# Cutting the last load of values of a decode attention kernel at 1/2 and 7/8 instead of 1/2 and 3/4

## The chip, the cores and the metric

The kernel runs on one core of one Trainium2 chip. The metric is the device time of one execution in microseconds (us). Times of a pair are compared within the same rounds on the same chip. Times inside an execution are counted from the start of its profiled span and rounded to hundredths, so a difference of two of them can be off by 0.01 us. The profile models the ends of matmuls; the starts of matmuls and of the casts behind them are recorded.

## The reference

```python
xn = _layernorm(x)                                   # x: 2 x 1 x 448, bfloat16
q  = (xn @ wq)                                       # 16 query heads of 256, 8 key/value heads
k, v = caches[:, :, Sk - 4096:, :]                   # the last 4096 of 32768 positions
p  = softmax(q k^T * 256 ** -0.5)
out = x + (p @ v) @ wo + mish_mlp(xn)                # one query position in each of 2 sequences
```

For each of 8 key/value heads and 2 sequences, 2 MB of keys and 2 MB of values are read once: 16 "heads" in the words of the kernel. With the weights some 78 MB are read for an output of 1.8 KB.

## The kernel before

Partition p holds 32 consecutive positions (T = 32) of 256 elements, that is 16 KB of keys and 16 KB of values per head. The loads stand in one queue, issued by SyncE. The parts here are the last head's values, the output weights `wo` behind them, and the products that use both.

```python
def load_v(i, cuts=(0, T)):                          # one load per part
    ...
    for lo, hi in zip(cuts, cuts[1:]):
        nc.sync.dma_start(out=t[:, lo:hi, :], in_=vin[:, lo:hi, :])

def load_wo(kvh, parts=1):                           # 448 KB for two query heads
    ...
    for u in range(parts):
        hs = slice(u * rep // parts, (u + 1) * rep // parts)
        nc.sync.dma_start(out=w[:, hs, :], in_=win[:, hs, :])

def values_fixed(i):                                 # the last four heads
    ...
    for t in range(T):                               # 2 matmuls for each t: 64 in all
        for c in range(ND):
            nc.tensor.matmul(po[:, c, :], lhsT=vv[:, t, c, :], rhs=pTv[:, th, 0:Q:HS], ...)
    scale_o(i, po)                                   # VectorE: oT = o / denominator

def mix(kvh):                                        # 16 matmuls, 8 for each query head h
    for h in range(rep):
        for c in range(ND):
            add(oT[:, c, h, :], w[:, h, c * D : (c + 1) * D], ...)

for i in range(NK + KA):                             # NK = 16 heads
    if i + 2 < NK:
        load_k(i + 2)
    if i < NK:
        load_v(i, (0, T) if i < NK - 1 else (0, T // 2, 3 * T // 4, T))
        ...
        if b == Bsz - 1:
            load_wo(kvh, parts=1 if i < NK - 1 else 2)
    ...

for n in range(NO):                                  # the close: four casts, one store
    copy = nc.vector.tensor_copy if n // 2 == 0 else nc.scalar.copy
    copy(out=res[:, n * DO : (n + 1) * DO], in_=part(n))
nc.sync.dma_start(out=out.flatten_outer_dims(), in_=res[:])
```

The softmax here doesn't subtract the row's maximum and nothing guards it: scores larger than these inputs give would overflow.

Of the kernel before, what the change touches and what calls it, by code (L numbers as in the profile page):

```python
# [34 lines left out]
def kernel(  # L35
# [26 lines left out]
    T = W // P  # L62
# [40 lines left out]
    def v_tile(n):  # L103
        t = v_pool.tile([P, T * Dh], BF16, tag="v", name="v")
        return t[:, 0:n]
# [150 lines left out]
    def build_q(i):  # L256
        kvh, b = heads[i]
        x, h0 = divmod(kvh * rep, HH)
        t = qdiag[i % NW]
        tv = t[:].rearrange("p (n e) c -> p n e c", e=NE)  # L260
        for j in range(NQ):
            rows = slice(j * Q, (j + 1) * Q)
            for e in range(NE):
                nc.gpsimd.tensor_copy(  # L264
                    out=tv[rows, :, e, j * Q : (j + 1) * Q : HS],
                    in_=qrep[rows, :, h0 : h0 + rep, e, x, b],
                )
# [56 lines left out]
    def dense_out():  # L324
        w2_sb = dense.pop("w2")
        for x in range(NX):
            for c in range(NF):
                add(act_bf[:, c, x, :], w2_sb[:, x, c, :])
# [6 lines left out]
    def load_k(i):  # L335
        kvh, b = heads[i]
        t = k_pool.tile([P, T * Dh], BF16, tag="k", name="k")
        nc.sync.dma_start(  # L338
            out=t[:], in_=A_k_cache[b, kvh, s0:Sk, :].rearrange("(p t) d -> p (t d)", p=P)
        )  # L340
        k_t[i] = t

    def load_v(i, cuts=(0, T)):
        kvh, b = heads[i]
        t = v_tile(T * Dh).rearrange("p (t d) -> p t d", t=T)
        vin = A_v_cache[b, kvh, s0:Sk, :].rearrange("(p t) d -> p t d", p=P)
        for lo, hi in zip(cuts, cuts[1:]):
            nc.sync.dma_start(out=t[:, lo:hi, :], in_=vin[:, lo:hi, :])
        v_t[i] = t

    def load_wo(kvh, parts=1):
        w = wo_pool.tile([P, rep, ND * D], BF16, tag="wo", name="wo")
        r0 = kvh * rep * Dh
        win = A_wo[r0 : r0 + rep * Dh, :].rearrange("(h p c) d -> p h (c d)", h=rep, p=P)
# [3 lines that stand above are left out]
        wo_t[kvh] = w  # L358

    def turn(s):  # L360
        kt = kt_pool.tile([P, TH * Dh], BF16, tag="kt", name="kt")
        i, half = divmod(s, NH)
        k = k_t[i] if half < NH - 1 else k_t.pop(i)
        nc.vector.transpose(  # L364
            out=kt[:].bitcast(FP32),
            in_=k[:, half * TH * Dh : (half + 1) * TH * Dh].bitcast(FP32),
        )
        kt_t[s] = kt

    def scores(s):  # L370
        i = s // NH
        ktv = kt_t.pop(s)[:].rearrange("p (t n c e) -> p n e t c", t=TH, n=NB, e=NE)
        psc = ps_sc.tile([P, TH, Q], FP32, tag="sc", name="sc")
        for n in range(NB):
            for e in range(NE):
                nc.tensor.matmul(  # L376
                    psc[:],
                    lhsT=qdiag[i % NW][:, n * NE + e, :],
                    rhs=ktv[:, n, e, :, :],
                    start=(n == 0 and e == 0),  # L380
                    stop=(n == NB - 1 and e == NE - 1),
                )
        p_sb = p_pool.tile([P, TH * Q], BF16, tag="p", name="p")
        if s % NH == 0:
            state["rs", i] = small.tile([P, NH], FP32, tag="rs", name="rs")
        nc.scalar.activation(  # L386
            out=p_sb[:],
            in_=psc[:].rearrange("p t c -> p (t c)"),
            func=ACT.Exp,
            scale=scale,  # L390
            accum_out=state["rs", i][:, s % NH : s % NH + 1],
        )
        p_t[s] = p_sb

    def turn_p(s):
        pT = p_pool.tile([P, TH * Q], BF16, tag="pT", name="pT", bufs=7)
        nc.vector.transpose(out=pT[:], in_=p_t.pop(s)[:])  # L397
        pT_t[s] = pT
        i, half = divmod(s, NH)
        if half != NH - 1:  # L400
            return
        rs = state.pop(("rs", i))
        sums = small.tile([P, rep], FP32, tag="sums", name="sums", bufs=4)
        nc.vector.tensor_scalar(  # L404
            out=sums[:], in0=hsel, scalar1=rs[:, 0:1], scalar2=None, op0=ALU.mult
        )
        nc.vector.scalar_tensor_tensor(  # L407
            out=sums[:], in0=hsel, scalar=rs[:, 1:2], in1=sums[:], op0=ALU.mult, op1=ALU.add
        )
        state["sums", i] = sums  # L410
# [13 lines left out]
    def values(i):  # L424

        po = ps_o.tile([NR, NP * Dh], FP32, tag="o", name="o")
        v = v_t.pop(i)
        state["rec", i] = denominator(i)
        for u in range(T // NP):
            half, uh = divmod(u, TH // NP)  # L430
            nc.tensor.matmul(  # L431
                po[:],
                lhsT=pT_t[i * NH + half][:, uh * NP * Q : (uh + 1) * NP * Q : HS],
                rhs=v[:, u * NP : (u + 1) * NP, :].rearrange("p t d -> p (t d)"),
                start=(u == 0),
                stop=(u == T // NP - 1),
            )
        o_sb = small.tile([NR, NP * Dh], FP32, tag="o_sb", name="o_sb", bufs=1)
        nc.scalar.copy(out=o_sb[:], in_=po[:])  # L439
        state["o", i] = o_sb  # L440
# [28 lines left out]
    def values_fixed(i):  # L469

        state["rec", i] = denominator(i)
        pq = ps_q.tile([P, NP * ND * NR], FP32, tag="q", name="q")
        po = pq[:, 0 : ND * rep].rearrange("p (c h) -> p c h", c=ND)
        vv = v_t.pop(i).rearrange("p t (m c) -> p t c m", c=ND)
        for t in range(T):
            half, th = divmod(t, TH)
            pTv = pT_t[i * NH + half][:].rearrange("p (t c) -> p t c", t=TH)
            for c in range(ND):
                nc.tensor.matmul(  # L479
                    po[:, c, :],  # L480
                    lhsT=vv[:, t, c, :],
                    rhs=pTv[:, th, 0:Q:HS],
                    start=(t == 0 and c == 0),
                    stop=(t == T - 1),
                    skip_group_check=True,
                )
        scale_o(i, po)
# [12 lines left out]
    NK = len(heads)  # L500
# [11 lines left out]
    def close(i):  # L512
        if i < NK - NFIX:
            finish(i)
        kvh, b = heads[i]
        if b == Bsz - 1:
            mix(kvh)

    for i in range(NK + KA):
        if i + 2 < NK:  # L520
            load_k(i + 2)
        if i < NK:
            load_v(i, (0, T) if i < NK - 1 else (0, T // 2, 3 * T // 4, T))
            kvh, b = heads[i]
            if b == Bsz - 1:
                load_wo(kvh, parts=1 if i < NK - 1 else 2)
            for half in range(NH):
                s = i * NH + half
                if s + 1 < NSTEP:
                    turn(s + 1)  # L530
                scores(s)
                if s >= 1:
                    turn_p(s - 1)
                if s == NSTEP - 1:
                    turn_p(s)
                if half == 0 and i > KA:
                    close(i - KA - 1)
            if i + 2 < NK:
                build_q(i + 2)
        if i == NK:  # L540
            close(i - KA - 1)
        if i == 0:
            dense_in()
        if i == 1:
            dense_out()
        if i >= KA:
            if i - KA < NK - NFIX:
                values(i - KA)
            else:
                values_fixed(i - KA)  # L550
        if i >= NK:
            close(i - KA)
# [37 lines left out]
```

## Time and profile before

| | before |
|---|---|
| time, first three runs | 190.46 us median (190.43 to 190.48) |
| profiled span | 188.7 us |
| DMA | 77.86 MB at a mean of 413 GB/s |
| last values landed | 184.27 us |
| second half of the last wo landed | 185.44 us |
| first cast | 185.86 us |

The first three rows are in the results and on the page. A landing is the last of the sixteen semaphore increments of a load, as the trace records it. The chain that ended last, from the trace of the kernel before (start us, length us, what), ran like this at the end:

```profile
158.66 25.61 DMA v<-in_A_v_cache_dram
184.27 0.05 issue
184.31 0.60 PE q L479 x16
184.91 0.02 issue
184.94 0.18 DVE oT L447
185.11 0.04 issue
185.16 0.79 PE psA L214 x15
185.94 0.23 ACT res L557
186.18 0.27 ACTq L585
```

This goes from the last values through their 16 matmuls, the scaling and the wo products to the close, and puts everything from 184.27 on the path. But the wo products stand as one piece of 0.79 us, and a wait inside that piece does not show. The prediction finds it in the timeline.

### The profile page before, as it was taken

The page shows a single profiled execution, that of the slowest core. Times are in us where ns is not written, and L with a number is a line of the kernel's source. Part 1 is how long each engine was busy: PE and PEld are TensorE (multiplying, and loading weights), DVE is VectorE, ACT ScalarE, POOL GpSimd, SP SyncE. Part 2 cuts the span into 40 slices and gives each one's busy share as a digit, 9 for nine tenths or more (in the row PEclk, how much of TensorE's full clock was granted, in tenths as well). Part 3 has the DMA queues.
Part 4 walks back from the last instruction along what each step waited for, and adds up shares of the span by engine and source line. Part 5 has one row for each costly group of instructions (what it writes and reads, how often), then busy time and mean ns, then how long its engine had stood idle before and what let it go on. Part 6 is the DMA issues. An engine that isn't in the chain of part 4 may idle for free.

```text
span 188.7 us, 2944 instructions
## 1 busy us (share of the span) xinstructions
PE 144.1 (76%) x1158; PEld 71.7 (38%) x1158; DVE 113.5 (60%) x195; ACT 32.5 (17%) x82; POOL 27.1 (14%) x139
## 2 busy tenths in 40 slices
PE   0152991788995799869985999769986999597782
PEld 0042390234442345334432434324533443254671
DVE  7805505997919392857649381939376673939401
ACT  2300110112212022111222112202311121211101
POOL 8004430033030022003030203003110300000000
PEclk9999995799999699988999699969998799969955
DMA  6999999999999999999999999999999999999991
GB/s 216 423 432 422 430 430 434 438 431 420 417 441 431 420 416 438 441 427 405 442 434 429 434 420 431 434 431 420 431 431 438 412 432 434 431 441 417 408 394 49
DMA packets 7816, 77.86 MB, mean 413 GB/s; under 512 B 757, under 2 KB 2809, under 8 KB 3322
## 3 DMA queue, kind: packets, MB, share of 16 engines
q1 hardware_dynamic: 7796, 77.66, 97.3%
q8 instruction: 9, 0.15, 0.3%
q14 instruction: 5, 0.04, 0.1%
q10 hardware_dynamic: 6, 0.01, 0.0%
HBM read 77.67 MB, written 0.00 MB: 412 GB/s over the span
## 4 chain that ended last, share of the span: by engine, by line
DMA 82%; DVE 11%; issue 2%; PE 2%; SPq 1%; ACT 0%; ACTq 0%
DMA k<-in_A_k_cache_dram 68%; DMA v<-in_A_v_cache_dram 14%; DVE kt L364 8%; DVE pT L397 2%; PE sc L376 1%; SPq L114 0%; PE psA L214 0%; SPq L338 0%; PE q L479 0%; SPq L280 0%; DVE sums L407 0%; SPq L275 0%; DVE sums L404 0%; DVE den_sb L320 0%; ACT p L386 0%
## 5 line engine op out<-in xcount | busy, mean ns | idle before, releaser
L364 DVE STREAM_TRANSPOSE kt<-k 128x2048 f32<-128x2048 f32 x32 | 73.4, 2296 | 50.6 <-DMA k<-in_A_k_cache_dram 49.6
L376 PE MATMUL sc<-kt,qdiag 128*128 128x512 bf16 x256 | 72.7, 433 | 17.6 <-DVE kt L364 15.8
L376 PEld LDWEIGHTS <-qdiag 128*128 128x128 bf16 x256 | 24.7, 105 | 57.2 <-issue 30.0
L431 PE MATMUL o<-v,pT 128*4 128x512 bf16 x192 | 43.4, 379 | 0.0
L264 POOL COPY qdiag<-qrep 32x8 bf16<-32x8 bf16 x128 | 23.1, 213 | 122.4 <-PE sc L376 107.6
L386 ACT ACTIVATE p<-sc 128x512 bf16<-128x512 f32 x32 | 19.1, 597 | 95.6 <-PE sc L376 93.1
L431 PEld LDWEIGHTS <-pT 128*4 128x4 bf16 x192 | 15.8, 87 | 21.8
L397 DVE STREAM_TRANSPOSE pT<-p 128x512 bf16<-128x512 bf16 x32 | 21.5, 672 | 1.1 <-ACT p L386 1.1
L439 ACT COPY o_sb<-o 4x512 f32<-4x512 f32 x12 | 6.9, 574 | 36.8 <-PE o L431 36.8
L214 PE MATMUL psA<-wo,oT 128*2 128x112 bf16 x128 | 3.8, 245 | 11.0 <-DVE oT L447 11.0
L479 PE MATMUL q<-pT,v 128*128 128x2 bf16 x256 | 7.6, 165 | 1.7 <-DMA v<-in_A_v_cache_dram 1.6
L460 PEld LDWEIGHTS q<-ident_f,o_sb 4*128 4x128 f32 x48 | 6.6, 206 | 5.1 <-issue 5.1
L479 PEld LDWEIGHTS <-v 128*128 128x128 bf16 x256 | 7.3, 101 | 2.0 <-DMA v<-in_A_v_cache_dram 2.0
L414 PEld LDWEIGHTS den<-sums,ones_f 128*128 128x128 f32 x32 | 6.8, 220 | 3.3 <-issue 1.7
L460 PE MATMUL q<-ident_f,o_sb 4*128 4x4 f32 x48 | 7.6, 261 | 0.0
L235 PE MATMUL qT_ps<-xs,v 128*128 128x4 bf16 x112 | 3.3, 166 | 4.8 <-DVE ones L201 2.8
L214 PEld LDWEIGHTS <-oT 128*2 128x2 bf16 x128 | 1.8, 87 | 11.9 <-DVE oT L447 11.7
L386 ACT ACTIVATION_READ_ACCUMULATOR p<-sc 128x1 f32 x32 | 6.2, 194 | 0.0
L177 PE MATMUL xnT_ps<-ident,xn_bf 2*128 2x2 bf16 x7 | 0.5, 167 | 6.3 <-DVE xn_bf L139 6.3
L414 PE MATMUL den<-sums,ones_f 128*128 128x2 f32 x32 | 5.1, 229 | 0.0
L235 PEld LDWEIGHTS <-v 128*128 128x128 bf16 x112 | 3.1, 104 | 5.0 <-issue 3.0
L462 DVE COPY osum<-q 128x4 f32<-128x4 f32 x12 | 1.9, 158 | 3.9 <-PE q L460 3.9
(52 smaller groups left out, 46.5 us busy)
## 6 DMA issues: line engine op xcount, KB each, us to landing
k<-in_A_k_cache_dram SPq DMA_DIRECT2D x16, 2048.0 KB, 31.5
v<-in_A_v_cache_dram SPq DMA_DIRECT2D x15, 2048.0 KB, 34.8
v<-in_B_w_dram SPq DMA_DIRECT2D x2, 1568.0 KB, 21.0
wo<-in_A_wo_dram SPq DMA_DIRECT2D x7, 448.0 KB, 31.5
v<-in_A_wq_dram SPq DMA_DIRECT2D x1, 2048.0 KB
v<-in_A_wq_dram SPq DMA_DIRECT2D x1, 1536.0 KB, 10.8
v<-in_A_v_cache_dram SPq DMA_DIRECT2D x1, 1024.0 KB, 29.1
v<-in_A_v_cache_dram SPq DMA_DIRECT2D x2, 512.0 KB, 27.4
```

Of the source, the lines that this page charges most:

```text
L214: nc.tensor.matmul(part(n), lhsT=lhsT, rhs=w[:, n * DO : (n + 1) * DO], start=start, stop=stop, tile_position=(0, n * Q), skip_group_check ...
L235: nc.tensor.matmul(qT_ps[:, hh, e, :], lhsT=wq_v[s][:, hh, e, :], rhs=xs[:, s, :, :].rearrange("p x b -> p (x b)"), start=(s == 0), stop=( ...
L264: nc.gpsimd.tensor_copy(out=tv[rows, :, e, j * Q : (j + 1) * Q : HS], in_=qrep[rows, :, h0 : h0 + rep, e, x, b],)
L364: nc.vector.transpose(out=kt[:].bitcast(FP32), in_=k[:, half * TH * Dh : (half + 1) * TH * Dh].bitcast(FP32),)
L376: nc.tensor.matmul(psc[:], lhsT=qdiag[i % NW][:, n * NE + e, :], rhs=ktv[:, n, e, :, :], start=(n == 0 and e == 0), stop=(n == NB - 1 and ...
L386: nc.scalar.activation(out=p_sb[:], in_=psc[:].rearrange("p t c -> p (t c)"), func=ACT.Exp, scale=scale, accum_out=state["rs", i][:, s % N ...
L397: nc.vector.transpose(out=pT[:], in_=p_t.pop(s)[:])
L414: nc.tensor.matmul(den[:], lhsT=ones_f[:], rhs=state.pop(("sums", i))[:], start=True, stop=True)
L431: nc.tensor.matmul(po[:], lhsT=pT_t[i * NH + half][:, uh * NP * Q : (uh + 1) * NP * Q : HS], rhs=v[:, u * NP : (u + 1) * NP, :].rearrange( ...
L439: nc.scalar.copy(out=o_sb[:], in_=po[:])
L460: nc.tensor.transpose(pqv[:, u, c, :], ov[:, u, c, :], ident_f[0:NR, 0:NR])
L479: nc.tensor.matmul(po[:, c, :], lhsT=vv[:, t, c, :], rhs=pTv[:, th, 0:Q:HS], start=(t == 0 and c == 0), stop=(t == T - 1), skip_group_chec ...
```

## The change

The intent is to shorten the work behind the last values. Only a quarter of the head, 16 matmuls, was left when its last load landed; with a smaller last part it is 8. The load before it grows from a quarter to three eighths.

```diff
-            load_v(i, (0, T) if i < NK - 1 else (0, T // 2, 3 * T // 4, T))
+            load_v(i, (0, T) if i < NK - 1 else (0, T // 2, 7 * T // 8, T))
```

## The prediction

> **What bounds the kernel now.** I read the page first: the engine totals, the strip of 40 slices, the chain that ended last. The lines that carry it:
>
> ```profile
> span 188.7 us, 2944 instructions
> DMA  6999999999999999999999999999999999999991
> DMA packets 7816, 77.86 MB, mean 413 GB/s; under 512 B 757, under 2 KB 2809, under 8 KB 3322
> ...
> DMA 82%; DVE 11%; issue 2%; PE 2%; SPq 1%; ACT 0%; ACTq 0%
> ```
>
> The DMA engines are at nine tenths or more from the second slice to the last but one, and the chain is 82% DMA. The kernel streams 77.86 MB and is bound by that. The change moves no byte, so only the end can give anything: the time between the last bytes and the stored result. So I read the timeline of the last six microseconds (start us, us, engine, line, operation, tiles, count, and in brackets the idle time before it and its releaser):
>
> ```profile
> 183.09 0.59 PE L479 MATMUL q<-pT,v 128*128 128x2 bf16 x16 [0.21 <-DMA v<-in_A_v_cache_dram]
> 184.31 0.50 PEld L479 LDWEIGHTS <-v 128*128 128x128 bf16 x16 [0.72 <-DMA v<-in_A_v_cache_dram]
> 184.31 0.59 PE L479 MATMUL q<-pT,v 128*128 128x2 bf16 x16 [0.63 <-DMA v<-in_A_v_cache_dram]
> 184.94 0.17 DVE L447 TENSOR_TENSOR oT<-q,rec 128x4 bf16<-128x4 f32 x1 [3.00 <-PE q L479]
> 185.15 0.18 PEld L214 LDWEIGHTS <-oT 128*2 128x2 bf16 x9 [0.34 <-DVE oT L447]
> 185.16 0.68 PE L214 MATMUL psA<-wo,oT 128*2 128x112 bf16 x16 [0.26 <-DVE oT L447]
> 185.49 0.10 PEld L214 LDWEIGHTS <-oT 128*2 128x2 bf16 x7 [0.15 <-issue]
> 185.86 0.56 DVE L557 CAST res<-psA 2x112 bf16<-2x112 f32 x2 [0.76 <-PE psA L214]
> 186.51 0.34 SPq L558 DMA_DIRECT2D out_dram<-res  x1
> ```
>
> The last head's values arrive in three parts and feed 32, 16 and 16 matmuls (two for each of 32 rows of a partition). The last quarter lands, 16 matmuls run, VectorE scales (oT), 16 matmuls multiply by the output weights wo, two engines cast, the store goes out. Read alone, this and the chain say that the tail after the last values (184.27 to the end) is the critical path, and that halving the last part shortens it.
>
> The line at 185.49 says otherwise. After nine weight loads the sequence stops for 0.15 us, then the other seven go; the gap is named "issue", which means that no releaser was inferred. The operands in the trace show it: matmul 9 of these 16 waits on the semaphore of the very last load, the second half of wo, which stands in the queue behind all values. The trace's semaphore records give the sixteenth and last increment of each of the last loads:
>
> - values, half: 181.82; first quarter: 183.04; last quarter: 184.26
> - wo, first half: 184.80; second half: **185.44**
>
> Matmul 9 starts at 185.48, 0.04 us after that. The last DMA, not the values, sets the end now.
>
> **What the Trainium skill says.** "DMA: Bandwidth & Descriptors", section "Queues, rings and completion order": on each DMA engine descriptors are consumed in ring order. The trace agrees: the five loads above land in the order of issue, about a queue's transfer time apart (512 KB in 1.22 us is 430 GB/s). A part that is cut elsewhere therefore does not let wo pass or hold it back. The same page, "Rules for kernel authors", asks for at least 1 MiB per DMA and warns mainly below 64 KB; the new last part has 256 KB. The trace decides how much that costs here: a packet of 4096 B takes 159 ns, 8192 B 309 ns, 12288 B 460 ns (medians), thus about 9 ns plus 0.0366 ns per byte. "TensorE: Matmul & The Clock Gate", section "Wait — 56ns, not 53.3ns?": start to start never drops below about 25 ns however small N is. The value matmuls with two columns agree, 26 to 27 ns apart, and do so at granted clock 1.0 and at the 0.5 of the end; the clock doesn't enter the sum.
>
> **The change part by part.**
> 1. *Instructions.* The compiled order is the same on PE, DVE, ACT and POOL; on SyncE two loads of 128x2048 elements become 128x3072 and 128x1024. No load is added, and the waits are the same. SyncE issued these loads at 153.8 and 158.7, some 25 us before they landed, held by waits on loads eight places earlier, which don't change. Issue: 0.
> 2. *Transfer.* 128 rows each of 4096 + 4096 B become 6144 + 2048 B: by the fit 234 + 84 = 318 ns for a row against 2 x 159 = 318. Each of 16 engines has 8 rows: difference 0. The last part still lands at 184.26 (the same last byte), the middle part at 183.04 + 0.61 = 183.65 (half of a quarter's 1.22 us).
> 3. *PE after the landings.* The middle part has 24 matmuls: 183.70 + 24 x 0.0267 = 184.34. Only then can the last 8 start, though their data landed 0.08 earlier: 8 x 0.0267 = 0.21, plus the 0.165 of one matmul less its gap, so the end is near 184.70 to 184.73, against 184.90. Halving the tail would give 0.21; the backlog of the larger middle part eats a little, leaving about 0.17 to 0.19 us.
> 4. *What follows.* oT runs from about 184.76 to 184.92 instead of 184.94 to 185.10, and the first eight wo matmuls start near 184.97 instead of 185.16; their weights landed at 184.80.
> 5. *The end.* The ninth wo matmul still waits for 185.44. It starts at 185.48, as before; the casts (185.86) and the store (186.51) stay where they are. The 0.18 us becomes a longer idle time ahead of matmul 9, 0.15 us now, about 0.33 us then.
>
> Sum: 0 + 0 - 0.18 + 0.18 = **0.00 us**.
>
> **The rivals.**
> *A: the tail is the bound.* The chain of waits ends in the values, and names no wo load. Then the 0.18 us reaches the end: 190.28 us, which is 0.1% faster. Against it stands the stop inside the run of wo matmuls.
> *B: smaller rows slow the DMA.* 2048 B rows might cost more than the fit says, or the uneven parts might spread worse over the 16 engines, whose increments for one load already lie 1.7 us apart. Since wo lands last, any such loss goes straight to the end. Twice the fitted 84 ns on 8 rows would add 0.7 us: 191.1. For it: nothing; the 1792 B rows of wo take 74 ns, on the fit.
> *C: PE's backlog becomes the bound.* If the middle part landed late, 24 matmuls at once would delay the rest. There are 0.33 us of room ahead of matmul 9, more than half of the 24 x 0.0267 = 0.64 us of the whole middle part, so a shift of 0.3 us would still be hidden. At the worst +0.1.
> *D: the granted clock of the end moves with the pattern of matmuls.* It is 0.5 from 178.9 on. At 1.0 the last eight wo matmuls (0.35 us) might end 0.1 us earlier.
>
> **Range and chances.** The sum gives 190.46 us, the time before. What can move it is small: A -0.18, D -0.1, C +0.1, B a few tenths at most likely, and the spread of runs, which is 190.43 to 190.48 here but on another chip or day may be 0.1 to 0.2%, 0.2 to 0.4 us. Predicted: 190.45 us; 8 in 10 between 190.2 and 190.8. Two per cent are 3.8 us, twenty times the largest term of any rival but B, so within 2%: 0.98; faster 0.01; slower 0.01.
>
> **What would show each step right or wrong.** Steps 1 and 2: the DMA strip and packets as before, a 6144 B packet near 234 ns and a 2048 B one near 84, the middle part landing near 183.65, the second half of wo near 185.44 on the same scale. Step 3: 24 and 8 value matmuls almost without a gap, where now two groups of 16 have 0.6 us between them. Steps 4 and 5: oT about 0.18 us earlier, the gap ahead of the ninth wo matmul grown to about 0.33, and the casts where they are. If instead the first wo matmul moves and the casts move with it, rival A holds and I misread the wait. If wo lands later by tenths, B holds. The prediction as a whole fails if the change disturbs the stream long before the end, where I see nothing that differs.

## The result

| | before | after |
|---|---|---|
| median, 6 runs each | 190.47 us (190.39 to 190.74) | 190.50 us (190.43 to 190.92) |
| ratio after / before | | 1.0004, 95% interval 0.9991 to 1.0017 |
| last values landed | 184.27 | 184.31 |
| last value matmul ended | 184.90 | 184.76 |
| oT started | 184.94 | 184.79 |
| second half of wo landed | 185.44 | 185.41 |
| ninth wo matmul started | 185.48 | 185.45 |
| first cast | 185.86 | 185.83 |

The time is the same. The interval reaches from 0.17 us faster to 0.32 us slower, so it only just excludes the 0.18 us of the prediction's rival A; the trace has to carry the answer. The page of the changed kernel:

```profile
span 188.7 us, 2944 instructions
DMA  6999999999999999999999999999999999999991
DMA packets 7816, 77.86 MB, mean 413 GB/s; under 512 B 757, under 2 KB 2809, under 8 KB 3322
...
DMA 88%; DVE 10%; PE 0%; issue 0%; SPq 0%; ACTq 0%; ACT 0%; DVEq 0%
```

The stream is as it was: as many packets, as many bytes, the same mean rate. The timeline of the end of the changed kernel (in this and the later timelines, lines of ScalarE's casts and some weight loads are left out):

```profile
183.74 0.93 PEld L479 LDWEIGHTS <-v 128*128 128x128 bf16 x32 [0.89 <-DMA v<-in_A_v_cache_dram]
183.74 1.01 PE L479 MATMUL q<-pT,v 128*128 128x2 bf16 x32 [0.81 <-DMA v<-in_A_v_cache_dram]
184.79 0.16 DVE L447 TENSOR_TENSOR oT<-q,rec 128x4 bf16<-128x4 f32 x1 [2.83 <-PE q L479]
185.01 0.18 PEld L214 LDWEIGHTS <-oT 128*2 128x2 bf16 x9 [0.34 <-DVE oT L447]
185.01 0.79 PE L214 MATMUL psA<-wo,oT 128*2 128x112 bf16 x16 [0.26 <-DVE oT L447]
185.45 0.10 PEld L214 LDWEIGHTS <-oT 128*2 128x2 bf16 x7 [0.26 <-issue]
185.83 0.56 DVE L557 CAST res<-psA 2x112 bf16<-2x112 f32 x2 [0.87 <-PE psA L214]
186.47 0.34 SPq L558 DMA_DIRECT2D out_dram<-res  x1
```

The two groups of 16 value matmuls have become one run of 32. oT and the first wo matmul come 0.15 us earlier. Then PE stops for 0.26 us ahead of the other seven weight loads, where it stopped for 0.15 before, and the cast stands where it stood, 0.03 us earlier as the weights are. This time the chain of waits of the changed kernel names the load:

```profile
168.47 16.93 DMA wo<-in_A_wo_dram
185.41 0.04 issue
185.45 0.46 PE psA L214 x8
185.91 0.23 ACT res L557
186.14 0.27 ACTq L585
```

Eight wo matmuls, not fifteen, are in the last piece: those that waited for the second half of the weights.

### The profile page after: what moved, and what is told of

The parts are those of the page before. It is cut to its first block, busy times and chain, and to the rows that moved or that the text cites. A ratio compares the mean times of both kernels' runs of the same rounds, so it can differ in the third digit from the quotient of the medians.

```text
span 188.7 us, 2944 instructions
## 1 busy us (share of the span) xinstructions
PE 144.6 (77%) x1158; PEld 72.1 (38%) x1158; DVE 113.5 (60%) x195; ACT 32.5 (17%) x82; POOL 27.3 (14%) x139
## 4 chain that ended last, share of the span: by engine, by line
DMA 88%; DVE 10%; PE 0%; issue 0%; SPq 0%; ACTq 0%; ACT 0%; DVEq 0%
DMA k<-in_A_k_cache_dram 75%; DMA wo<-in_A_wo_dram 9%; DVE kt L364 7%; DMA v<-in_A_wq_dram 4%; DVE pT L397 2%; PE psA L214 0%; DVE sums L407 0%; DVE sums L404 0%; SPq L348 0%; ACTq L585 0%; ACT res L557 0%; DVE rec L418 0%; DVEq L364 0%
## 5 line engine op out<-in xcount | busy, mean ns | idle before, releaser
L376 PE MATMUL sc<-kt,qdiag 128*128 128x512 bf16 x256 | 70.7, 424 | 17.1 <-DVE kt L364 14.5
L431 PE MATMUL o<-v,pT 128*4 128x512 bf16 x192 | 46.1, 395 | 0.0
L376 PEld LDWEIGHTS <-qdiag 128*128 128x128 bf16 x256 | 24.0, 103 | 54.3 <-issue 25.1
L214 PE MATMUL psA<-wo,oT 128*2 128x112 bf16 x128 | 3.3, 219 | 11.1 <-DVE oT L447 11.0
L414 PEld LDWEIGHTS den<-sums,ones_f 128*128 128x128 f32 x32 | 7.8, 249 | 3.6 <-issue 1.7
L414 PE MATMUL den<-sums,ones_f 128*128 128x2 f32 x32 | 5.7, 247 | 0.0
L120 DVE CAST ident_f<-ident 32x32 f32<-32x32 bf16 x1 | 3.3, 3286 | 1.3 <-POOL ident masks.py:199 1.3
```

Of the source, the lines that this page charges most:

```text
L214: nc.tensor.matmul(part(n), lhsT=lhsT, rhs=w[:, n * DO : (n + 1) * DO], start=start, stop=stop, tile_position=(0, n * Q), skip_group_check ...
L376: nc.tensor.matmul(psc[:], lhsT=qdiag[i % NW][:, n * NE + e, :], rhs=ktv[:, n, e, :, :], start=(n == 0 and e == 0), stop=(n == NB - 1 and ...
L414: nc.tensor.matmul(den[:], lhsT=ones_f[:], rhs=state.pop(("sums", i))[:], start=True, stop=True)
L431: nc.tensor.matmul(po[:], lhsT=pT_t[i * NH + half][:, uh * NP * Q : (uh + 1) * NP * Q : HS], rhs=v[:, u * NP : (u + 1) * NP, :].rearrange( ...
```

## The experiments

Theory W: the second half of the last wo load, which stands last in the queue, sets the end, and the finer cut gains time that turns into waiting for it. Theory A: the values' path sets the end, and the finer cut gains nothing on it. Theory D: the cut changes what the DMA engines do. A later one, L, concerns the closing sequence. These letters belong to the experiments; the prediction's rivals A to D are others (its A says that a gain does reach the end, its B is close to this D, its D is the granted clock).

All numbers beside a kernel's name are median times, beside the kernel before in the same rounds: 190.59 us for the first four, 190.52 us for the other seven. All eleven came out "same" by the rule of 2%; what matters are tenths of a microsecond, so intervals and traces are read instead. "Tail" below is the time from the landing of the last values to the first cast, in the one profiled execution of each. It is the better measure here, since it leaves out when the stream happened to end: before 1.59 us, after 1.52 us.

### The weights ahead of the values

```diff
+            kvh, b = heads[i]
+            if i == NK - 1:
+                load_wo(kvh, parts=2)
             load_v(i, (0, T) if i < NK - 1 else (0, T // 2, 3 * T // 4, T))
-            kvh, b = heads[i]
-            if b == Bsz - 1:
-                load_wo(kvh, parts=1 if i < NK - 1 else 2)
+            if b == Bsz - 1 and i < NK - 1:
+                load_wo(kvh)
```

wo_first_quarter:

> The kernel before (half, quarter, quarter), but the last head's output weights are loaded ahead of its values, so that the values are the last to land. Theory W (the last load of output weights hides the end of the values' work): the last values then land where the weights landed, 1.17 us later, near 185.4; from that landing to the start of the ninth wo matmul it takes what it takes in the kernel before without the wait (0.67 to oT, 0.22 to the first wo matmul, 0.06 to the ninth: 0.95 us) in place of 0.04. So the ninth wo matmul no longer waits and starts near 186.4: 0.9 us slower, about 191.35 us. Theory A (the values' path sets the end anyway, and the change gains nothing because cutting finer gains nothing): the end follows the values here as well, also about +0.9; the pair with the next run tells the theories apart.

wo_first_eighth, the same with `7 * T // 8`:

> The same order with the change's cut (half, three eighths, eighth). Theory W: now the values' path is bare, and the cut must show: 8 matmuls less after the landing, less PE's backlog, oT about 0.15 to 0.2 us earlier against the last landing; 0.7 us slower than before, 0.15 to 0.2 us faster than the run wo_first_quarter (191.15 to 191.2 us). Theory A: no difference between these two runs, in the trace neither.

wo_first_quarter: 191.56 us, ratio 1.0053 (1.0040 to 1.0067). wo_first_eighth: 191.34 us, ratio 1.0040 (1.0027 to 1.0052). The timeline of wo_first_quarter, then that of wo_first_eighth:

```profile
185.35 0.59 PE L479 MATMUL q<-pT,v 128*128 128x2 bf16 x16 [0.65 <-DMA v<-in_A_v_cache_dram]
185.97 0.17 DVE L447 TENSOR_TENSOR oT<-q,rec 128x4 bf16<-128x4 f32 x1 [3.88 <-PE q L479]
186.19 0.54 PE L214 MATMUL psA<-wo,oT 128*2 128x112 bf16 x16 [0.26 <-DVE oT L447]
186.76 0.56 DVE L559 CAST res<-psA 2x112 bf16<-2x112 f32 x2 [0.62 <-PE psA L214]
```

```profile
184.74 1.08 PE L479 MATMUL q<-pT,v 128*128 128x2 bf16 x32 [0.83 <-DMA v<-in_A_v_cache_dram]
185.86 0.17 DVE L447 TENSOR_TENSOR oT<-q,rec 128x4 bf16<-128x4 f32 x1 [4.01 <-PE q L479]
186.08 0.54 PE L214 MATMUL psA<-wo,oT 128*2 128x112 bf16 x16 [0.26 <-DVE oT L447]
186.65 0.56 DVE L559 CAST res<-psA 2x112 bf16<-2x112 f32 x2 [0.62 <-PE psA L214]
```

The wo matmuls run in one piece of 0.54 us, with no stop: nothing waits for weights. The last values landed at 185.31 and 185.41, so the tails are 1.45 and 1.24 us: the finer cut is worth 0.21 us once the values' path is bare (nothing else holds up the work behind the values), and the medians differ by 0.22. That is W; A wanted no difference. (The intervals of the two ratios against before overlap, so the trace carries this more than the times do.) Both kernels are slower, by 0.7 to 1.0 us. What lands last should be what has the least work behind it: eight matmuls behind wo, a whole chain behind the values.

### The weights left out

```diff
-            if b == Bsz - 1:
-                load_wo(kvh, parts=1 if i < NK - 1 else 2)
+            if b == Bsz - 1 and i < NK - 1:
+                load_wo(kvh)
...
-        w = wo_t.pop(kvh)
+        w = wo_t[min(kvh, Hkv - 2)]
```

no_wo_quarter:

> Wrong result on purpose: the last head's output weights are not loaded at all, and those of the pair of heads before it are used in their place. The cut is that of the kernel before (half, quarter, quarter). Theory W: the values land where they did (the weights stood behind them in the queue), and the ninth wo matmul follows the eighth at once, near 185.22 in place of 185.48: 0.26 us faster, 190.2. Theory A: the last load of weights costs nothing now; no change beyond 0.05 us.

no_wo_eighth, the same with `7 * T // 8`:

> Wrong result on purpose, as no_wo_quarter, with the change's cut (half, three eighths, eighth). Theory W: what was hidden comes out: 0.15 to 0.2 us faster than no_wo_quarter, 0.4 to 0.45 us faster than before, 190.0 to 190.05. Theory A (the finer cut gains nothing): the same as no_wo_quarter.

Both use wrong weights for the last pair of heads. The comparison with the reference accepted the outputs all the same, so that comparison would not find an error of this kind.

no_wo_quarter: 190.26 us, ratio 0.9985 (0.9972 to 0.9997). no_wo_eighth: 190.07 us, ratio 0.9979 (0.9967 to 0.9992). The timeline of no_wo_eighth:

```profile
184.04 1.02 PE L479 MATMUL q<-pT,v 128*128 128x2 bf16 x32 [0.84 <-DMA v<-in_A_v_cache_dram]
185.10 0.16 DVE L447 TENSOR_TENSOR oT<-q,rec 128x4 bf16<-128x4 f32 x1 [2.95 <-PE q L479]
185.31 0.54 PE L214 MATMUL psA<-wo,oT 128*2 128x112 bf16 x16 [0.26 <-DVE oT L447]
185.89 0.56 DVE L557 CAST res<-psA 2x112 bf16<-2x112 f32 x2 [0.62 <-PE psA L214]
```

The stop is gone. The tails are 1.46 us (values landed at 184.23, cast at 185.69) and 1.29 us (184.60, 185.89). So the cut gains 0.17 us without the weights (the medians differ by 0.19, and here too the intervals overlap), and the wait for the weights costs 1.59 - 1.46 = 0.13 us before the change and 1.52 - 1.29 = 0.23 us after it. W holds in kind. In size, 0.13 is half of the 0.26 that was expected of no_wo_quarter, although the median moved by just those 0.26. The rest has another source. In the profiled executions the span is 0.38 us shorter: the values landed 0.04 us earlier, the wait is gone (0.13), and from the issue of the store to the end of the program it takes 2.00 us (no_wo_eighth 2.02) where the kernel before takes 2.21. The last two experiments take that up.

### How large the last part may be

Four runs change only the cuts: three make the last part larger, the fourth makes it as small as it goes. In the table, the medians of last_half and last_seven_eighths belong to the rounds in which the kernel before took 190.59 us, that of the change to those with 190.47.

```diff
-(0, T // 2, 3 * T // 4, T)
+(0, T // 4, T // 2, T)          # last_half
+(0, T // 16, T // 8, T)         # last_seven_eighths
+(0, T // 2, 5 * T // 8, T)      # last_three_eighths
+(0, T // 2, 31 * T // 32, T)    # last_32nd
```

> Cuts at a quarter and a half, so that the last part is half the head: 32 matmuls after the last landing. Theory W: the end is the later of two paths. Values: 184.31 + 32 x 0.0267 + 0.14 = 185.30, oT from 185.34 to 185.50, first wo matmul 185.56, ninth 185.62; weights: 185.48. So it sticks out by 0.14: +0.14 us, and no stop ahead of the ninth wo matmul. Theory A (each matmul after the last landing counts): 16 matmuls more than before, +0.43 us. A third, D (the cut changes what the DMA engines do, in either direction): the second half of wo lands elsewhere than 1.17 us after the last values.

> Cuts at a sixteenth and an eighth: the last part is seven eighths, 56 matmuls after the last landing. Theory W: 184.31 + 56 x 0.0267 + 0.14 = 185.95, oT until 186.15, ninth wo matmul near 186.27 against 185.48: +0.8 us, 191.25. Theory A: 40 matmuls more than before, +1.07 us, 191.5. D: as above.

> Cuts at a half and five eighths: the last part is three eighths, 24 matmuls after the last landing. Theory W: 184.31 + 24 x 0.0267 + 0.14 = 185.09, oT until 185.29, first wo matmul 185.35, eighth 185.41; the ninth still waits for the weights at 185.48, 0.07 us. So 0.0 us against before: a larger last part costs nothing up to here. Theory A: 8 matmuls more, +0.21 us.

> Cuts at a half and 31 of 32: the last part is one row in 32, 512 B for a partition and 64 KB in all, and the middle part 15/32. Theory W: 0.0 us, since the weights still end it. The middle part lands near 181.82 + 30 x 0.0763 = 184.11 and PE has 30 matmuls of backlog then, so oT starts later than in the change, near 185.15, and the ninth wo matmul still waits until 185.48. Theory D (small rows slow the stream): the second half of wo lands later, by some tenths if a row of 512 B costs much more than the 9 + 0.0366 x 512 = 28 ns that the fit of packets gives; if the fit holds, no later.

| run | last part | median us | ratio (95% interval) | values landed | wo landed | first cast | tail |
|---|---|---|---|---|---|---|---|
| last_32nd | 1/32 | 190.67 | 1.0009 (0.9997 to 1.0022) | 184.22 | 185.32 | 185.93 | 1.71 |
| after | 1/8 | 190.50 | 1.0004 (0.9991 to 1.0017) | 184.31 | 185.41 | 185.83 | 1.52 |
| before | 1/4 | | 1 | 184.27 | 185.44 | 185.86 | 1.59 |
| last_three_eighths | 3/8 | 190.70 | 1.0008 (0.9994 to 1.0021) | 184.25 | 185.38 | 185.93 | 1.68 |
| last_half | 1/2 | 190.78 | 1.0017 (1.0005 to 1.0030) | 184.25 | 185.43 | 186.14 | 1.89 |
| last_seven_eighths | 7/8 | 191.56 | 1.0052 (1.0039 to 1.0064) | 184.70 | 185.78 | 187.23 | 2.53 |

The bare tail of a quarter is 1.46 us (no_wo_quarter). Adding 0.0267 us for each further matmul gives 1.46 + 8 x 0.0267 = 1.67 for three eighths, 1.89 for a half and 2.53 for seven eighths: the three measured tails to 0.01 us. Of the five cuts from an eighth up, only the quarter and the eighth lie above their bare tails (1.46 and 1.29), and both have the cast 0.42 us after the landing of the weights. So in these five the end follows one rule: the first cast comes at the later of two times, the values' landing plus their bare tail, and the weights' landing plus 0.42 us. Under A alone the quarter would have its bare tail too, and a half would have cost 0.43 us; the cast came 0.28 us later than before. (Nothing shows what 1/32 would have bare; a third load sets its end, see below.)

The expectations were too low for three of these runs. last_half was to cost 0.14 and cost 0.2 (medians) to 0.3 us (means, and the cast); last_seven_eighths was to cost 0.8 and cost 0.97, between that and the 1.07 of A, because the room is only 0.13 us; last_three_eighths was to end with the weights, and its cast came 0.13 us after what they alone allow (185.38 + 0.42), 0.07 later than before, which the times do not resolve. The reason is in the timeline of last_three_eighths:

```profile
184.30 0.80 PE L479 MATMUL q<-pT,v 128*128 128x2 bf16 x24 [0.19 <-DMA v<-in_A_v_cache_dram]
185.14 0.17 DVE L447 TENSOR_TENSOR oT<-q,rec 128x4 bf16<-128x4 f32 x1 [2.48 <-PE q L479]
185.36 0.55 PE L214 MATMUL psA<-wo,oT 128*2 128x112 bf16 x16 [0.26 <-DVE oT L447]
185.93 0.26 DVE L557 CAST res<-psA 2x112 bf16<-2x112 f32 x1 [0.62 <-PE psA L214]
```

The ninth of the wo matmuls started at 185.50, 0.14 us after the first, not 0.06 as I had taken from the spacing of the first eight; and from there to the last end it is 0.40 us, not the 0.36 it takes after a wait. Run in one piece, the sixteen take 0.54 to 0.55 us. That is 0.12 us more on the values' path than my sum had.

The trace of the kernel before could have told this. The same sixteen instructions run after every pair of heads. At 165.31 us, at a granted clock of 0.5, they took 0.54 us, the ninth 0.14 us after the first; at 178.04 us, at a granted clock of 1.0, they took 0.37 us, the ninth 0.10 us after the first. In the thirteen traces together, all 82 groups that ran wholly at 1.0 took 0.37 us, and all 12 that ran wholly at 0.5 without a wait took 0.54 to 0.55 us. So this work goes with the granted clock, although no run set the clock on purpose.

last_32nd speaks against D. A packet of 512 B took 27 ns, where the fit of the prediction gives 28, and the second half of wo landed at 185.32 us, no later than before: no extra cost of a load of 64 KB shows in this full queue. (Landings of one queue differ between executions by up to 0.25 us, see two_parts, so a small cost would not show.) But the last part can be too small:

```profile
184.09 1.02 PE L479 MATMUL q<-pT,v 128*128 128x2 bf16 x32 [0.78 <-DMA v<-in_A_v_cache_dram]
185.14 0.17 DVE L447 TENSOR_TENSOR oT<-q,rec 128x4 bf16<-128x4 f32 x1 [2.48 <-PE q L479]
185.36 0.54 PE L214 MATMUL psA<-wo,oT 128*2 128x112 bf16 x16 [0.26 <-DVE oT L447]
```

The middle part, 15/32, landed at 184.04, only 0.18 us before the last. PE began the 32 matmuls of both at 184.09, which is later than the 183.74 of the change, and oT came at 185.14. The expectation saw that time rightly and missed what it does: it is 0.35 us later than in the change, and the cast came 0.19 us after what the weights alone allow (185.32 + 0.42), 0.07 later than before.

### The closing sequence

Each load that SyncE or ScalarE issues, and the store, uses the next of eight semaphores in turn. At the end SyncE waits for all of them, in five instructions of fixed order; the store's own semaphore is checked by whichever of them its place falls to. Dropping two loads in no_wo_quarter had moved it from the second of these waits to the last.

```diff
# one_fewer_quarter
-(0, T // 2, 3 * T // 4, T)
+(0, 3 * T // 4, T)
# two_parts: the same, and
-    nc.scalar.dma_start(out=b1_sb[:, :], ...)
+    nc.gpsimd.dma_start(out=b1_sb[:, :], ...)
# two_fewer_eighth: the changed kernel, and
-    nc.scalar.dma_start(out=x_bf[:, :], ...)
-    nc.scalar.dma_start(out=b1_sb[:, :], ...)
+    nc.gpsimd.dma_start(out=x_bf[:, :], ...)
+    nc.gpsimd.dma_start(out=b1_sb[:, :], ...)
```

> The kernel before with the last head's values in two loads (three quarters, one quarter) in place of three, so that one load fewer is made and the store of the result falls to the semaphore of the next place in the ring of eight (the one that the closing sequence checks in its third wait rather than in its second). Theory W: PE has 48 + 16 matmuls after the landings at 183.04 and 184.27: 183.09 + 64 x 0.0267 + 0.14 = 184.94, oT until 185.14, ninth wo matmul ready near 185.34, still before 185.48: the work itself ends as before, 0.0 us. Theory L (the closing waits come in a fixed order, each 0.07 us after the one before, and those that stand behind the store's are paid after its landing): from the store's landing to the end of the program 0.07 us less than the 1.06 us of before, 190.4 to 190.5 us beside 190.5; without L nothing.

> The same two loads of values, and the small bias b1 is loaded from the GpSimd queue, which has its own semaphores: two loads fewer in the ring, so that the store falls to the place that is checked last. Theory L: from the store's landing to the end 0.85 us in place of 1.06, as in no_wo_quarter and no_wo_eighth, so 0.2 us faster than before at the same work, 190.3 us. Without L (the shorter end of the two kernels without the weights came from the missing transfer): 1.06 us as before, 190.5.

> The changed kernel (half, three eighths, eighth), with both small inputs x and b1 loaded from the GpSimd queue: again two loads fewer in the ring. Theory L: 0.85 us from the store's landing to the end, 0.2 us faster than the changed kernel, 190.3 us. The same loads of values and weights as in the change, so the ninth wo matmul waits for the weights as there. What could spoil it: x comes later through GpSimd, but the first matmuls that need it run near 6 us while the projection waits for its weights; an added wait on the GpSimd queue's semaphore at the close, 0.07 us.

| run | median us | ratio (95% interval) | store issued to end of program |
|---|---|---|---|
| before | 190.52 | 1 | 2.21 |
| one_fewer_quarter | 190.42 | 0.9995 (0.9981 to 1.0008) | 2.15 |
| two_parts | 190.41 | 0.9995 (0.9982 to 1.0007) | 2.06 |
| two_fewer_eighth | 190.50 | 1.0001 (0.9988 to 1.0013) | 2.08 |
| no_wo_eighth | 190.07 | 0.9979 (0.9967 to 0.9992) | 2.02 |

The traces agree with L in direction: 0.06 us for one place, 0.13 to 0.15 us for the last place, where 0.2 was expected. The 0.06 alone proves little: in wo_first_quarter and wo_first_eighth, with the store's semaphore in the same place as before, this stretch took 2.17 us, 0.04 less. In the two kernels that use the GpSimd queue the close also had a sixth wait, and the clearing of semaphores took 0.14 us in place of 0.10, which eats a part. The times do not resolve it: none of the three is shown to be faster than before. In two_parts the second half of wo landed at 185.69 in the profiled execution, 0.25 us later than before, with the same bytes in the queue; such differences between executions are as large as all that is sought here. The other finding of one_fewer_quarter and two_parts is that two parts do as well as three: the weights landed at 185.55 and 185.69, the first cast came 0.43 us after that in both, and the tail of the values stayed hidden.

So no version is shown to beat both kernels. The last eighth is sound, and so is the quarter.

## Why the prediction was right

**The stream bounds the kernel, and no byte moves.** Right: the same packets, the same 413 GB/s.

**Steps 1 and 2, instructions and transfer.** Right (but for a slip: the first of the two loads was issued 29 us before it landed, not 25). Packets of 6144 and 2048 B took 234 and 84 ns (medians), as the fit said. The middle part landed at 183.70 (183.65 was predicted), the last part at 184.31 (184.26), wo at 185.41 (185.44). No loss of rival B's kind is seen, nor in last_32nd with its smaller rows.

**Step 3, PE behind the landings.** Right. From the landing of the last values to the end of the last value matmul it took 0.63 us before and 0.45 us after: 0.18 less, 0.17 to 0.19 predicted. The two pairs of experiments put the gain at 0.17 and 0.21 us when it is bare.

**Step 4, oT and the first wo matmul.** Right, 0.15 us earlier on the clock and 0.18 against the landing.

**Step 5, the wait for the weights.** Right in kind: the ninth wo matmul started 0.04 us after its weights landed, in both kernels, and taking the weights off the end or out of it made the gain visible. What was mis-sized is the room. The text gives 0.15 us of idle time before and about 0.33 after, and rival C is weighed against that 0.33. The idle time after was 0.26, since the weights happened to land 0.07 us nearer to the values; and the room that counts was 0.13 us before and 0.23 after, because sixteen wo matmuls in one piece take 0.54 us, which the sum did not have. The prediction also says that the clock doesn't enter the sum. That holds for the value matmuls, 26 ns apart at a granted clock of 1.0 and 27 at 0.5, but not for the sixteen wo matmuls (0.37 and 0.54 us). For this change that made no difference: the shorter values' path could only lengthen a wait that was already there. For last_32nd, last_three_eighths and last_half it did.

**The rivals.** A, that the gain reaches the end, is refuted by the result: oT came 0.15 us earlier, the cast only the 0.03 us by which the weights landed earlier. The experiments' theory A, that the finer cut gains nothing on the values' path, is refuted by both pairs. C is not seen in the change (PE was done in time) but is what last_32nd shows. D: the granted clock at the end was 0.5 in both kernels, so it did not come into play.

**What stays open.** Why the end of the stream varies by tenths between executions with the same queue.

## What to carry to other kernels

When a kernel is bound by its loads to the end, list the landings of the last few loads and ask of each what work stands behind it; the end is the latest of landing plus work, and shortening another of them only lengthens a wait. A chain of waits that merges many instructions into one piece can hide such a wait: look for a stop inside the piece, and for the operand that its first instruction waits for. Take the time of such a piece from a place in the trace where it runs undisturbed at the same granted clock, not from the spacing of its first instructions. Put last in the queue what has the least work behind it, and cut loads no finer than the next path allows: a very small last part leaves its work in the part before it.

## What the Trainium skill lacked or had wrong

- "DMA: Bandwidth & Descriptors", "Rules for kernel authors", says of transfers under 64 KB that one pays mostly overhead, and asks for 1 MiB. At that edge, behind a full queue, no overhead was seen: a load of 64 KB in rows of 512 B had packets of 27 ns, on the same line as the large ones (about 9 ns plus 0.0366 ns per byte), and the load behind it landed no later (185.32 us against 185.44).
- The same page, "Anatomy of one DMA — SWDGE (gpsimd) path", gives a fixed cost of about 2.0 us, most of it the receipt, for that path; for the SyncE queue I found no such split. Here it was 0.42 us from the end of the last packet of wo (185.02) to its last increment (185.44; 0.33 us in the changed kernel), and 1.15 us from the issue of the small store to its landing.
- The same page, "Latency and other measured facts", names two of the sixteen engines as usually slower, and ties that to the GpSimd path. Here, on the SyncE queue, the sixteen increments of one load fell into two groups: for the half of the last head in the kernel before, eight from 180.02 to 180.91 and eight from 181.52 to 181.82 us (in the two quarters behind it seven and nine). Which engines these were the trace's increments do not say; a load lands with the slower group.
- "TensorE: Matmul & The Clock Gate", "Wait — 56ns, not 53.3ns?", gives a floor of about 25 ns from start to start, with a measured example at the full clock alone. The value matmuls, of two columns, were 26 ns apart at a granted clock of 1.0 and 27 ns at 0.5.
- No page that I read says what the place of the store's semaphore among the closing waits of a program does. With that place the time from the issue of the store to the end changed from 2.21 us to between 2.00 and 2.15, in single executions; kernels with the place unchanged lay between 2.17 and 2.22.
